# HGRN2 outer-product attention and a PReLU network on one core: where the off-diagonal products are put in PSUM and in TensorE's order

## The chip, the core and the metric

One Trainium2 chip, and one of its cores. A core has a matrix engine (TensorE; in the profile PE for its matmuls and PEld for its weight loads), VectorE (DVE), ScalarE (ACT), GpSimd (POOL) and SyncE (SP), which only issues transfers here. Matmuls write to PSUM, a memory of eight banks with 512 float32 columns each on 128 partitions; VectorE and ScalarE read them from there. Engines run on their own and wait for each other by semaphores. The metric is the time of one launch in microseconds on the device; the kernel before took 618.38 us (median of three runs, 618.32 to 619.0).

## The reference

```python
f = 1.0 / (1.0 + np.exp(-f_logit))
for t in range(S):                                  # S = 768, B, H, D = 4, 8, 48
    state = f[:, :, t, :, None] * state + np.einsum('bhd,bhe->bhde', k[:, :, t], v[:, :, t])
    y[:, :, t] = np.einsum('bhd,bhde->bhe', q[:, :, t], state)
...
x = attn_out.transpose(0, 2, 1, 3).reshape(B * S, H * D)       # 3072 x 384
h = x @ w_in                                                   # 384 x 2048
g = np.maximum(h, 0.0) + alpha * np.minimum(h, 0.0)
return (g @ w_out).astype(np.float32)                          # 2048 x 384
```

The recurrence can be written as a masked matrix of scores within a chunk of time plus a carried state. For a time t and an earlier time s of one chunk the score is q[t]·k[s] times the product of the forget gates between them.

## The kernel before

**Steps.** Time is cut in six chunks of 128, and the batch of four in two pairs. A step is one chunk of one pair, so there are 12 steps (numbered 0 to 11 here); the first two hold the first chunk (`c == 0`), and "from the third step on" means steps 2 to 11 (`c > 0`). Each step has four parts, written as generators: `prepare` (L258, key P or Q), `carry` (L432, key O), `attend` (L506, key S), and `network` (L609, key n), the dense layers on a step's rows.

**Order.** TensorE, VectorE and ScalarE work in exactly the order in which the program writes their instructions. This order is the string at L31 to L37: each key runs the generator of that kind up to its next `yield`. `n` is the network of the step before, `Q` the preparation of the step after. `FIRST` holds the first four steps, `USUAL` the rest. In a usual step TensorE's order is

- the first `S`: scores `raw0` (L520) and `qu0` (L535) of the first batch; two pieces of `n` (12 `ph` matmul instructions each, L618);
- the second `S`: `raw1`, `qu1` of the second batch; one `n`;
- the first `O`: `off` (L444); one `n`; the second `O`: `pd` (L484), the new part of the state; four more `n`;
- `pa`, `pb` (L657, the second dense layer), `py` (L574, the attention's output, in the third to fifth `S`), and the other products of L657.

**Scores.** `raw` has the scores between times of the same or a neighbouring group of four, 80 columns of every 128, `qu` those further apart within a block of 32. VectorE puts both into the tile `ad` with masked copies (four at L526, seven at L541 for each batch), and ScalarE copies `ad` into the big score tile `A` (L563). `off` holds scores between the two blocks of 32 in a half chunk of 64: `kh` (keys scaled to the end of their block, written at L374) against `q3[.., 2]` (queries scaled from the start of theirs, L368). ScalarE copies `off` into `A` with four copies (L462). Four more copies (L419) bring the carried part. `py` multiplies `A` with the values.

**Instructions.** A float32 matmul of the program is two matmuls and two weight loads on the chip: 64 of each for the 32 `off` matmuls of a step, and 64 for a batch's `raw` or `qu`. [...]

**PSUM.** `pair` (L122) hands out two banks at a time from a pool of two such pairs, in turn. A usual step of before asks for seven pairs: raw0, qu0, raw1, qu1, off, pd, py. `network` has four single banks.

**ScalarE and VectorE beside it.** A piece of `n` gives ScalarE one `neg` (L623, reads `ph`) and VectorE two `gate` (L625); every fourth piece adds four `S` (L702). `Q` has on ScalarE L279 to L282, L314 and L419, and on VectorE L290 to L415. The second `O` gives VectorE L494 and L498. On the queues, POOL loads `k`, `q`, `f` and `v` (L266, L276), and SP moves `kt` to `ksn` (L427), which `pd` reads.

Of the kernel before, what the change touches and what calls it, by code (L numbers as in the profile page):

```python
# [18 lines left out]
DB = 32  # L19
MASKED = (1, 0)  # L20

U = 2
CH = 64
NC2 = C // CH
# [6 lines left out]
FIRST = (  # L31
        "P5 a2 P a O w S w a w a2 S Q S O S w Q2 S Q2 S w",
        "a2 w2 n O b w n b2 S P v2 n2 S b v Q n b n O S2 v n b v n Q2 b v Q b n S v2 W Q W S n2 W n",
        "n S P n2 S W n W n O Q n3 O S Q n S Q n Q S2 Q n3",
        "S n3 P S Q S n O n O n4 Q S Q S Q n S Q n Q n2",
)
USUAL = "S n2 S n O n O n Q n3 Q n Q S3 n Q S n Q n Q n"  # L37

def flat(first, usual, steps=12):
    out = []  # L40
# [18 lines left out]
def kernel(  # L59
# [30 lines left out]
    nc = tc.nc  # L90
    B, NC, _, HP, _ = qT.shape
# [7 lines left out]
    W = U * HP * C  # L99
# [13 lines left out]
    QW = QO.pop()  # L113
# [8 lines left out]
    def pair(name):  # L122
        return psa.tile([128, 2, 512], F32, tag="pair", name=name)
# [39 lines left out]
    for m in range(1, NB):  # L163
        lo = UO[m] + (4 if m == 1 else 0)
        n = NB - m
# [4 lines left out]
    for half in range(2):  # L170
        for m in range(1, NQ):
            n = NQ - m
# [7 lines left out]
    A = const.tile([128, U, H, C], F32, tag="A", name="A")  # L180
# [67 lines left out]
    def rows(par):  # L248
        return slice(64 * par, 64 * par + D)
# [182 lines left out]
    def carry(bp, c, x):  # L432

        i = f"{bp}_{c}"
        q3, ks, kh, f64 = (x[n] for n in ("q3", "ks", "kh", "f64"))
        off = pair(f"off_{i}")
        for u in range(U):
            for hp in range(HP):
                for cc in range(NC2):
                    g = (u * HP + hp) * NC2 + cc  # L440
                    o = (u * HP + hp) * DB
                    for par in range(2):
                        r_ = rows(par)
                        nc.tensor.matmul(off[CH * cc:CH * cc + DB, par, o:o + DB],  # L444
                                         lhsT=kh[r_, g], rhs=q3[r_, g, 2], start=True, stop=True)
        if not c:
            for u in range(U):
                for hp in range(HP):
                    for j in range(NJ):
                        g = (u * HP + hp) * NJ + j  # L450
                        o = U * HP * DB + (u * HP + hp) * 16
                        for par in range(2):
                            r_ = rows(par)
                            nc.tensor.matmul(off[DB * j:DB * (j + 1), par, o:o + 16], lhsT=x["k16"][r_, g],
                                             rhs=x["q16"][r_, g], start=True, stop=True)
            for u in range(U):
                o = U * HP * DB + u * HP * 16
                nc.scalar.copy(ad[:, u, :, :, 16:DB], off[:, :, o:o + HP * 16].rearrange("p r (h t) -> p r h t", h=HP))
        for cc in range(NC2):
            s_ = slice(CH * cc, CH * cc + DB)  # L460
            for par in range(2):
                nc.scalar.copy(A[s_, :, par * HP:(par + 1) * HP, CH * cc + DB:CH * (cc + 1)],  # L462
                               off[s_, par, 0:U * HP * DB].rearrange("p (u h t) -> p u h t", u=U, h=HP))


        if not c:
            pk = pair(f"pk_{i}")
            for u in range(U):
                for hp in range(HP):
                    a = (u * HP + hp) * NC2  # L470
                    nc.tensor.transpose(pk[:, u, hp * 128:(hp + 1) * 128], ks[:, a:a + 2].rearrange("p c s t -> p (c s t)"), ident)
            ksn = x["ksn"] = work.tile([128, U, HP * 128], F32, tag="ksn", name=f"ksn_{i}", bufs=1)
            for u in range(U):
                nc.scalar.copy(ksn[:, u], pk[:, u])
        yield
        pd = pair(f"pd_{i}")
        ksn = x["ksn"]
        for u in range(U):
            for hp in range(HP):
                for cc in range(NC2):  # L480
                    for par in range(2):
                        o = (u * HP + hp) * D
                        s_ = halves(cc)[0]
                        nc.tensor.matmul(pd[rows(par), cc, o:o + D],  # L484
                                         lhsT=ksn[s_, u, hp * 128 + 64 * par:hp * 128 + 64 * par + D],
                                         rhs=vs[bp][s_, cc, u, (2 * hp + par) * D:(2 * hp + par + 1) * D], start=True, stop=True)

        def moved(cc):

            of, to = halves(cc)[1], halves(1 - cc)[1]  # L490
            was, then = (vs[bp][p, a, :, 0:DM].rearrange("p u (h e) -> p u h e", e=D)
                         for p, a in ((of, cc), (to, 1 - cc)))
            if c or cc:
                nc.vector.tensor_tensor(then, was, f64[of].unsqueeze(3).broadcast_to((D, U, H, D)), ALU.mult)  # L494
            for par in range(2):
                now = pd[rows(par), cc, 0:U * HP * D].rearrange("p (u h e) -> p u h e", u=U, e=D)
                if c or cc:
                    nc.vector.tensor_tensor(then[:, :, par:H:2], then[:, :, par:H:2], now, ALU.add)  # L498
                else:
                    nc.scalar.copy(then[:, :, par:H:2], now)  # L500

        x["moved"] = moved
        moved(0)
        yield

    def attend(bp, c, x):  # L506

        i = f"{bp}_{c}"
        k, k4, us = (x[n] for n in ("k", "k4", "us"))


        QL, QS = (UW, UW) if c else (VW, C)
        for u in range(U):
            raw = pair(f"raw{u}_{i}")
            for hp in range(HP):
                for j in range(NJ):
                    g = (u * HP + hp) * NJ + j
                    for par in range(2):
                        r_ = rows(par)
                        nc.tensor.matmul(raw[DB * j:DB * (j + 1), par, hp * C:hp * C + QW],  # L520
                                         lhsT=k[r_, g * DB:(g + 1) * DB], rhs=qd[r_, g], start=True, stop=True)
            adu = ad[:, u].rearrange("p r h (i t) -> p (r h) i t", t=4)
            rv = raw.rearrange("p r (h x) -> p (r h) x", h=HP)
            for d in range(4):
                n = 4 - d
                nc.vector.copy_predicated(  # L526
                    adu[:, :, :, d:4], mraw[:, d, :, d:4].bitcast(I32).unsqueeze(1).broadcast_to((128, H, NB, n)),
                    rv[:, :, QO[d]:QO[d] + NB * n].rearrange("p h (i t) -> p h i t", t=n))
            qu = pair(f"qu{u}_{i}")
            for hp in range(HP):  # L530
                for j in range(NJ):
                    g = (u * HP + hp) * NJ + j
                    for par in range(2):
                        r_ = rows(par)
                        nc.tensor.matmul(qu[DB * j:DB * (j + 1), par, hp * QS + 4:hp * QS + QL],  # L535
                                         lhsT=k4[r_, g * DB:(g + 1) * DB], rhs=us[r_, g, 4:QL], start=True, stop=True)
            if c:
                for m in range(1, NB):
                    lo = UO[m] + (4 if m == 1 else 0)
                    n = DB - 4 * m  # L540
                    nc.vector.copy_predicated(  # L541
                        ad[:, u, :, :, 4 * m:DB],
                        mquad[:, lo:lo + n].bitcast(I32).unsqueeze(1).unsqueeze(1).broadcast_to((128, 2, HP, n)),
                        qu[:, :, 0:HP * UW].rearrange("p r (h x) -> p r h x", h=HP)[:, :, :, lo:lo + n])
            else:
                qv = qu.rearrange("p r (h x) -> p (r h) x", h=HP)
                adh = ad[:, u].rearrange("p r h (a t) -> p (r h) a t", a=2)
                for m in range(1, NQ):
                    n = 4 * (NQ - m)
                    lo = 4 if m == 1 else VO[m]  # L550
                    hi = lo + (DB - 4 if m == 1 else 2 * n)
                    to, of, by = ad[:, u].rearrange("p r h t -> p (r h) t")[:, :, 4:DB], qv[:, :, lo:hi], mhalf[:, lo:hi]
                    by = by.bitcast(I32).unsqueeze(1).broadcast_to((128, H, hi - lo))
                    if m > 1:
                        to = adh[:, :, :, 4 * m:16]
                        of, by = (t.rearrange("p h (a t) -> p h a t", a=2) for t in (of, by))
                    nc.vector.copy_predicated(to, by, of)
            yield

        for u in range(U):  # L560
            for j in range(NJ):
                s_ = slice(DB * j, DB * (j + 1))
# [5 lines left out]
        for u in range(U):  # L568
            for hp in range(HP):
                for cc in range(NC2):  # L570
                    for par in range(2):
                        hd = 2 * hp + par
                        o = hp * C + CH * cc
                        nc.tensor.matmul(py[64 * par:64 * par + 64, u, o:o + CH],  # L574
                                         lhsT=vs[bp][:, cc, u, hd * D:hd * D + 64],
# [223 lines left out]
```

## Time and profile before

| what | value |
|---|---|
| median of three runs | 618.38 us |
| span of the profiled execution | 616.6 us |
| instructions | 19078 |
| PE, PEld busy | 587.9 us, 525.1 us |
| DVE, ACT, POOL busy | 496.0 us, 245.7 us, 62.8 us |
| TensorE clock granted | 1.00 in the steps from 100 us on |
| off L444: weight loads, matmuls | 768 each, 102 to 156 ns and 192 to 260 ns long |
| A<-off L462 | 48 copies of 32x256, 360 ns median |
| ad<-mraw,raw L526 | 96 masked copies, 441 ns |
| POOL k L266 waits for PE raw L520 | 208.0 us, 11 times |

The span runs from the first instruction of the program to the last; the median lies 1.8 us above it, for what is around the program in a launch. A busy time counts when an instruction is in flight, so that small matmuls which run side by side count once. The line numbers are those of the kernel before. In the lines that tell of waiting, `<-` names what ended the wait; `issue` means that nothing in the profile was waited for.

### The profile page before, as it was taken

The page shows a single profiled execution, that of the slowest core. Times are in us where ns is not written, and L with a number is a line of the kernel's source. Part 1 is how long each engine was busy: PE and PEld are TensorE (multiplying, and loading weights), DVE is VectorE, ACT ScalarE, POOL GpSimd, SP SyncE. Part 2 cuts the span into 40 slices and gives each one's busy share as a digit, 9 for nine tenths or more (in the row PEclk, how much of TensorE's full clock was granted, in tenths as well). Part 3 has the DMA queues.
Part 4 walks back from the last instruction along what each step waited for, and adds up shares of the span by engine and source line. Part 5 has one row for each costly group of instructions (what it writes and reads, how often), then busy time and mean ns, then how long its engine had stood idle before and what let it go on. Part 6 is the DMA issues. An engine that isn't in the chain of part 4 may idle for free.

```text
span 616.6 us, 19078 instructions
## 1 busy us (share of the span) xinstructions
PE 587.9 (95%) x8220; PEld 525.1 (85%) x8220; DVE 496.0 (80%) x997; ACT 245.7 (40%) x466; POOL 62.8 (10%) x117
## 2 busy tenths in 40 slices
PE   3568999999999999999999999999999999999997
PEld 3457867898899899899889899899889889889997
DVE  7599898899898798798798798798898889762251
ACT  5687852441641361262261261352352343223110
POOL 9120010001010011001001001001001000000000
PEclk9998999999999999999999999999999999999999
DMA  9965532014414214214313313413413301201000
GB/s 302 368 236 180 161 86 54 35 37 120 89 31 75 70 39 105 67 35 98 78 34 93 83 35 90 86 35 87 89 35 86 89 2 27 55 1 27 27 1 26
DMA packets 68116, 50.43 MB, mean 82 GB/s; under 512 B 47168, under 2 KB 60608, under 8 KB 68032
## 3 DMA queue, kind: packets, MB, share of 16 engines
q1 hardware_dynamic: 56656, 25.01, 15.6%
q0 software_dynamic: 6864, 22.35, 13.0%
q10 hardware_dynamic: 4512, 1.85, 1.7%
q8 instruction: 65, 1.06, 0.7%
q14 instruction: 19, 0.16, 0.1%
HBM read 36.21 MB, written 4.72 MB: 66 GB/s over the span
## 4 chain that ended last, share of the span: by engine, by line
PE 67%; DVE 19%; ACT 9%; issue 4%; DMA 1%; ACTq 0%; SPq 0%; DVEq 0%
PE ph L618 27%; PE pc L657 9%; PE pa L657 6%; PE pd L657 5%; PE pe L657 4%; PE po L638 3%; PE raw L520 3%; DVE gate L625 3%; PE qu L535 3%; ACT A L563 3%; DVE S L702 3%; DVE qd L287 3%; PE py L574 3%; ACT us L314 2%; PE pb L657 2%
## 5 line engine op out<-in xcount | busy, mean ns | idle before, releaser
L618 PE MATMUL ph<-xT,w_in_sb 128*128 128x256 f32 x1152 | 261.2, 383 | 0.7 <-DVE Csum L661 0.7
L618 PEld LDWEIGHTS ph<-xT,w_in_sb 128*128 128x128 f32 x1152 | 215.9, 190 | 33.2 <-issue 2.4
L623 ACT ACTIVATE neg<-ph 128x512 f32<-128x512 f32 x96 | 57.2, 596 | 198.2 <-PE ph L618 157.1
L625 DVE SCALAR_TENSOR_TENSOR gate<-neg,om,ph 128x256 f32<-128x256 f32 x192 | 82.3, 477 | 52.3 <-ACT neg L623 52.1
L657 PE MATMUL pc<-t,S 128*128 128x192 f32 x352 | 61.7, 329 | 0.0
L657 PE MATMUL pa<-w_out_sb,gate 128*128 128x192 f32 x352 | 61.3, 327 | 0.1
L657 PEld LDWEIGHTS pa<-w_out_sb,gate 128*128 128x128 f32 x352 | 57.9, 190 | 1.0 <-DVE gate L625 0.4
L657 PEld LDWEIGHTS pc<-t,S 128*128 128x128 f32 x352 | 57.3, 190 | 0.6
L526 DVE COPY_PREDICATED ad<-mraw,raw 128x256 f32<-128x256 int32 (+1 forms) x96 | 42.4, 441 | 10.7 <-PE raw L520 8.2
L541 DVE COPY_PREDICATED ad<-mquad,qu 128x224 f32<-128x224 int32 (+6 forms) x140 | 42.0, 300 | 6.2
L419 ACT COPY A<-q 48x512 f32<-48x512 f32 x44 | 27.2, 617 | 36.4 <-DVE q L368 35.9
L563 ACT COPY A<-ad 32x256 f32<-32x256 f32 x96 | 38.5, 401 | 1.4
L330 DVE TENSOR_TENSOR us<-us,fs 128x768 f32<-128x768 f32 (+5 forms) x60 | 36.7, 612 | 0.0
L678 ACT ACTIVATE o<-pa 128x192 f32<-128x192 f32 x11 | 3.6, 330 | 75.2 <-PE pa L657 65.4
L661 DVE SCALAR_TENSOR_TENSOR Csum<-pc,Csum 128x192 f32<-128x192 f32 x22 | 7.8, 356 | 29.8 <-PE pc L657 29.6
L574 PEld LDWEIGHTS py<-A,vs 128*64 128x64 f32 x768 | 25.7, 145 | 6.1 <-issue 2.8
L702 DVE TENSOR_TENSOR S<-gate 128x512 f32<-128x512 f32 x44 | 30.3, 688 | 0.8
L574 PE MATMUL py<-A,vs 128*64 128x64 f32 x768 | 28.7, 232 | 1.9 <-ACT vs L500 0.9
L657 PE MATMUL pd<-w_out_sb,S 128*128 128x192 f32 x176 | 30.4, 326 | 0.0
L657 PE MATMUL pb<-t,gate 128*128 128x192 f32 x176 | 30.4, 326 | 0.0
L657 PE MATMUL pe<-w_out_sb,S 128*128 128x192 f32 x176 | 30.4, 326 | 0.0
L520 PEld LDWEIGHTS raw<-qd,k 48*32 48x32 f32 x1536 | 18.5, 109 | 13.5 <-issue 11.1
(101 smaller groups left out, 744.3 us busy)
## 6 DMA issues: line engine op xcount, KB each, us to landing
w_out_raw<-in_w_out SPq DMA_DIRECT2D x8, 767.8 KB, 5.3
w_in_raw<-in_w_in SPq DMA_DIRECT2D x8, 767.2 KB, 12.1
q<-in_qT POOLq DMA_DIRECT2D x11, 512.0 KB, 4.2
f<-in_fT POOLq DMA_DIRECT2D x11, 512.0 KB, 4.5
k<-in_kT POOLq DMA_DIRECT2D x11, 512.0 KB, 4.8
out<-o SPq DMA_DIRECT2D x24, 192.0 KB, 3.0
vs<-in_v POOLq DMA_DIRECT2D x22, 192.0 KB, 4.8
ksn<-kt SPq DMA_DIRECT2D x80, 32.0 KB, 2.0
```

What stands on the lines that cost most here:

```text
L330: nc.vector.tensor_tensor(us[:, :, UO[m]:UO[m] + 4 * n].rearrange("p g (i r) -> p g i r", r=4), us[:, :, skip:skip + 4 * n].rearrange("p g ...
L419: nc.scalar.copy(A[halves(cc)[1], :, par * HP:(par + 1) * HP, CH * cc:CH * (cc + 1)], q3[rows(par)].rearrange("p (u h c) s t -> p u h c (s ...
L520: nc.tensor.matmul(raw[DB * j:DB * (j + 1), par, hp * C:hp * C + QW], lhsT=k[r_, g * DB:(g + 1) * DB], rhs=qd[r_, g], start=True, stop=True)
L526: nc.vector.copy_predicated(adu[:, :, :, d:4], mraw[:, d, :, d:4].bitcast(I32).unsqueeze(1).broadcast_to((128, H, NB, n)), rv[:, :, QO[d]: ...
L541: nc.vector.copy_predicated(ad[:, u, :, :, 4 * m:DB], mquad[:, lo:lo + n].bitcast(I32).unsqueeze(1).unsqueeze(1).broadcast_to((128, 2, HP, ...
L563: nc.scalar.copy(A[s_, u, :, s_], ad[s_, u].rearrange("p r h t -> p (r h) t"))
L574: nc.tensor.matmul(py[64 * par:64 * par + 64, u, o:o + CH], lhsT=vs[bp][:, cc, u, hd * D:hd * D + 64], rhs=A[:, u, par * HP + hp, CH * cc: ...
L618: nc.tensor.matmul(ph[:, j * T:(j + 1) * T], lhsT=w_in_sb[:, kt, m * 128:(m + 1) * 128], rhs=xT[:, kt], start=(kt == 0 and j == 0), stop=( ...
L623: nc.scalar.activation(neg, phv, AF.Relu, scale=-1.0)
L625: nc.vector.scalar_tensor_tensor(gate[:, m % NH, m // NH], neg[:, j], om[:, m:m + 1], phv[:, j], ALU.mult, ALU.add)
L657: nc.tensor.matmul(to[:, 0:DH], lhsT=of(f), rhs=by(f), start=(f == 0 and not more), stop=(f == NH - 1), skip_group_check=True)
L702: nc.vector.tensor_tensor(to, x_, y_, op)
```

## The change

From step 2 on `off` has no pair of banks of its own. Directly after the `raw` matmuls of a batch, `attend` issues that batch's 16 `off` matmuls (32 instructions) into the 32 columns behind the 80 that `raw` uses, in the same two banks. The two ScalarE copies of that batch to `A` come after its four masked copies of L526, and each takes 32 x 256 elements as before. `carry` has only one `yield` left in these steps, and the order has one `O` less. Steps 0 and 1 are as they were.

```diff
-        "n S P n2 S W n W n O Q n3 O S Q n S Q n Q S2 Q n3",
-        "S n3 P S Q S n O n O n4 Q S Q S Q n S Q n Q n2",
+        "n S P n2 S W n W n Q n3 O S Q n S Q n Q S2 Q n3",
+        "S n3 P S Q S n2 O n4 Q S Q S Q n S Q n Q n2",
 )
-USUAL = "S n2 S n O n O n Q n3 Q n Q S3 n Q S n Q n Q n"
+USUAL = "S n2 S n2 O n Q n3 Q n Q S3 n Q S n Q n Q n"
...
     def carry(bp, c, x):
...
-        off = pair(f"off_{i}")
...
         if not c:
+            off = pair(f"off_{i}")
+            for u in range(U):
...
+            for cc in range(NC2):
+                s_ = slice(CH * cc, CH * cc + DB)
...
-        yield
+            yield
         pd = pair(f"pd_{i}")
...
     def attend(bp, c, x):
...
+            if c:
+                gap = raw.rearrange("p r (h x) -> p r h x", h=HP)[:, :, :, QW:QW + DB]
+                for hp in range(HP):
+                    for cc in range(NC2):
+                        g = (u * HP + hp) * NC2 + cc
+                        for par in range(2):
+                            r_ = rows(par)
+                            nc.tensor.matmul(gap[CH * cc:CH * cc + DB, par, hp],
+                                             lhsT=kh[r_, g], rhs=q3[r_, g, 2], start=True, stop=True)
...
+            if c:
+                for cc in range(NC2):
+                    s_ = slice(CH * cc, CH * cc + DB)
+                    nc.scalar.copy(A[s_, u, :, CH * cc + DB:CH * (cc + 1)].rearrange("p (r h) t -> p r h t", r=2),
+                                   gap[s_])
```

In `carry` the loops of `off` and of its four copies move unchanged under `if not c`. In `attend` the four masked copies of L526 stand between the two added parts.

## The prediction

> **Forecast: slower, 621.7 us.** I read the page, then TensorE's order of time, then who waits for whom.
>
> **What bounds it now.**
>
> ```profile
> span 616.6 us, 19078 instructions
> ...
> PE 587.9 (95%) x8220; PEld 525.1 (85%) x8220; DVE 496.0 (80%) x997; ACT 245.7 (40%) x466; POOL 62.8 (10%) x117
> ...
> q8 instruction: 65, 1.06, 0.7%
> ```
>
> TensorE is the bound. The last line will matter: a queue brings instructions, 65 packets, 1.06 MB, so 16 KB each; TensorE's 16,440 instructions and 248 waits, over 65, make 257 instructions per packet. TensorE in step 7, by time (start, length, what):
>
> ```profile
> 339.47 5.45 PE L618 MATMUL ph<-xT,w_in_sb 128*128 128x256 f32 x24
> 344.85 0.92 PE L520 MATMUL raw<-qd,k 48*32 48x80 f32 x64
> 345.54 1.07 PE L535 MATMUL qu<-us,k 48*32 48x112 f32 x64
> 346.54 2.86 PE L618 MATMUL ph<-xT,w_in_sb 128*128 128x256 f32 x12
> 349.32 0.76 PE L444 MATMUL off<-q,kh 48*32 48x32 f32 x64
> 350.01 2.86 PE L618 MATMUL ph<-xT,w_in_sb 128*128 128x256 f32 x12
> 352.80 1.22 PE L484 MATMUL pd<-vs,ksn 64*48 64x48 f32 x64
> ```
>
> One section starts as the last ends, nothing is waited for.
>
> **The gain in a usual step.** By starts, 12 `ph` take 2.78 us on either side of `off`, 24 in one piece 5.38: joining them saves 2.78 + 2.79 - 5.38 = 0.19. `off` costs 350.01 - 349.32 = 0.69. Behind `raw` its 64 matmuls cost 64 times the pace of a small matmul in a stream: 9.0 ns (between the starts of `off` itself), 10.9 (`raw`, 0.69/64), 15 (`qu` in the first half of a step, its slowest). That is 0.58, 0.70 or 0.96; I take 0.61, near `off`'s own row. Net 0.19 + 0.69 - 0.61 = 0.27 gained per step; ends -0.08 and +0.30.
>
> **Does it reach the end?** Yes in steps 4 to 11. From the fourth `gate` on, VectorE and ScalarE set the pace up to `py` (TensorE idles there 0.2 to 0.4 us), but that stretch starts with a wait for TensorE:
>
> ```profile
> 353.58 0.87 DVE L625 SCALAR_TENSOR_TENSOR gate<-neg,om,ph 128x256 f32<-128x256 f32 x2 [2.16 <-ACT neg L623]
> ```
>
> The gain lies ahead of it, so the stretch moves too. Eight steps: 8 x 0.27 = 2.15.
>
> **The copies on ScalarE** keep their count and size. What waits is new. Whether they may read beside L526 the trace can't show; if not, the second batch's start when L526 ends, about 348.5 in step 7, and take 4 x 0.36 / 2 = 0.72. Behind them queues `neg` of the next `ph`, due at 349.8: 0.5 to spare, or 2 if they may. `raw1` needs the first pair free at 345.1 and has it at 342.1; `pd` needs the second at 352.5 and has it at 349.3. L526 itself waits 0.3 longer for `off`, under the `gate` before it. The removed pair leaves every reuse as far away as it was. No transfer is added; SP and POOL keep their order, and `k`'s load (behind raw1) moves with TensorE. In one step `pd` waited 0.29 for `ksn`, which `py`'s idle time swallowed (`py` 2.08 instead of 2.37). All this I cost at 0; should the `neg` be late by x, TensorE loses x less the 2.16 of the row above.
>
> [...]
>
> **Steps 2 and 3 are different.** VectorE's waits from 110.5 to 150 us, and TensorE's from 100 (sum, times, longest):
>
> ```profile
> DVE gate L625 <- ACT neg L623: 1.3, 1, 1.3
> ```
>
> ```profile
> PE ph L618 <- DVE Csum L661: 0.7, 1, 0.7
> ```
>
> VectorE waits for TensorE once, before the third `gate` (110.62), then never; TensorE waits for it at the end. `off` (116.92) lay under that stretch. Now half of it is ahead of the third `ph`: +0.29, all on the path. In step 3 ScalarE's two copies stand before L279 to L282, which feed L287; VectorE is then 0.5 later, eats the 0.5 that the gate before `pa` has to spare, and most of that step's gain: -0.1 (ends -0.6, +0.1).
>
> **The cost: TensorE outruns its instructions.** In the first steps nothing hides it. Weight loads of step 0:
>
> ```profile
> 26.32 0.34 PEld L520 LDWEIGHTS raw<-qd,k 48*32 48x32 f32 x20 [1.27 <-issue]
> 26.50 0.17 PEld L535 LDWEIGHTS qu<-us,k 48*32 48x32 f32 x2
> 26.54 0.17 PEld L520 LDWEIGHTS raw<-qd,k 48*32 48x32 f32 x1
> 26.55 0.13 PEld L535 LDWEIGHTS qu<-us,k 48*32 48x32 f32 x1
> 26.60 0.19 PEld L520 LDWEIGHTS raw<-qd,k 48*32 48x32 f32 x4
> 26.63 1.08 PEld L535 LDWEIGHTS qu<-us,k 48*32 48x32 f32 x61
> 29.23 0.75 PEld L520 LDWEIGHTS raw<-qd,k 48*32 48x32 f32 x38 [1.52 <-issue]
> 32.24 0.34 PEld L520 LDWEIGHTS raw<-qd,k 48*32 48x32 f32 x21 [2.27 <-issue]
> ```
>
> It stops in the middle of `raw`, waiting for nothing. From one such stop (26.32) to the next (32.24) go 127 pairs and 2 waits: 256 instructions, one packet. Step 1 again, in the 128 loads of L454 behind `off`:
>
> ```profile
> 51.57 0.57 PEld L454 LDWEIGHTS off<-us 48*32 48x32 f32 x53 [1.46 <-issue]
> ```
>
> Three packets and no other stop lie between. The trace's list of DMA packets has the ones that ended the three stops: they started at 23.57, 29.77, 48.88 and took 1.28, 1.11, 1.40; TensorE went on 1.3 to 1.5 after each. So a block of 256 is fetched when the one before is entered: some 0.6 to 1.1 us until its packet starts, 0.9 to 1.5 for the packet, 1.37 after it, 3.3 in all. A block of small matmuls alone lasts 1.4. A stream of 256 (`raw`, `qu`) always has `ph` in its block; one of 320 can hold a whole block. Counting on from 51.57 in blocks of 256, in the new order:
>
> - Step 2, first batch: a block starts at the 60th instruction of `raw0`, the next 256 later, six before `qu0` ends. Its packet stands in the trace: 103.96, 1.29 long, usable at 106.6. TensorE is there at 102.77 + 0.70 + 0.29 + 0.78 = 104.5: stop of 2.1, ahead of the third `ph`, so in full.
> - Step 5, second batch: block start at the 72nd of `raw1`; stop 3.7 - 2.4 = 1.3 after it.
> - Step 10, second batch: at the 63rd; 3.6 - 1.8 = 1.8.
>
> Elsewhere TensorE's sequencer enters the block under `ph`, some 36 instructions ahead, or `ph` fills it. Ends: 0 (the fetch keeps up) and 5 stops of 1.7 (steps 3 and 7, whose starts lie within 16 instructions of such a place, too).
>
> [...] The stops at 26.32, 32.24 and 51.57, one block each, speak for a single block ahead.
>
> **Sum.** +0.29 + 2.1 (step 2) - 0.1 (step 3) - 2.15 + 1.3 + 1.8 = +3.3 on 616.6: span 619.9. The median lies 1.8 above the span: 618.4 + 3.3 = **621.7**.
>
> **Rivals.**
>
> 1. The fetch keeps up: +0.29 - 0.1 - 2.15 = -2.0: **616.4**, faster. For it: no such stop from step 2 on in the trace of before, in 20 streams. Against: none of those streams holds a whole block. It decides while a packet is usable within 1.4 us of entry. 13 in 100.
> 2. Only step 2 stops, since later blocks lie otherwise (waits added to TensorE's queue shift them): +0.29 + 2.1 - 0.1 - 2.15 = +0.1: **618.5**. The count holds to step 2, where the code is the old one; further on each wait moves it by one. 15 in 100.
> 3. The joined `ph` bring nothing in steps 4 to 11, since VectorE's stretch binds whole steps: +0.29 + 2.1 - 0.1 + 3.1 = +5.4: **623.8**. Against: its 2.16 of waiting in each step. With it more stops, five: 621.7 + 2 x 1.7 = 625.1. 17 in 100.
>
> The forecast has 55 in 100, with its own range 620.2 to 623.5. The whole range reaches down to rival 2 and up past 3's first time: 617.9 to 624.6. Within 0.2% (1.24 us, about what a measurement tells from no change) lies rival 2 and a little of the others: 0.16; faster, rival 1: 0.14; slower 0.70.
>
> **What would show it.** After: L444 only in steps 0 and 1 (128); in step 2 a gap of 2 us, released by `issue`, near the end of `qu0`; two more of 1 to 2 us inside or just behind long streams; in the other steps `ph` in blocks of 24 from `qu1` to `pd`, each step 0.27 shorter. Wrong if no such gap shows, or if ScalarE's copies make `gate` wait.

## The result, and the profile after

The median of the changed kernel is 625.65 us (four runs, 624.1 to 627.51) beside 618.35 for the kernel before, a ratio of 1.0124 (95% interval 1.0103 to 1.0146): slower, as forecast, but by 7.3 us and not by 3.3, and outside the range, which ended at 624.6. In the profiled execution the span is 7.6 longer. The page of the kernel after, its lines on busy time and on the queue that brings instructions (packets, MB, share):

```profile
span 624.2 us, 19088 instructions
...
PE 589.5 (94%) x8220; PEld 527.7 (85%) x8220; DVE 496.4 (80%) x997; ACT 248.0 (40%) x466; POOL 63.0 (10%) x117
...
q8 instruction: 65, 1.06, 0.8%
```

The work is the same to the instruction on every engine, and TensorE is busy for 1.6 us more while the span grows by 7.6. So TensorE idles. Its waits from 95 to 625 us (sum, times, longest):

```profile
PE qu L549 <- issue: 4.9, 3, 1.7
PE py L588 <- ACT A L577: 1.1, 6, 0.3
PE ph L632 <- DMA ksn<-kt: 0.7, 1, 0.7
...
```

The first line is new: three times TensorE stops inside `qu` (L549 now) and waits for nothing that the profile shows. The third line is a fourth such stop, in step 7: `ph` does not read `ksn`, and a transfer of it happened to end then. The weight loads show where they stand (start, length, what, idle time before), in steps 2, 5, 7 and 10:

```profile
104.04 0.78 PEld L549 LDWEIGHTS qu<-us,k 48*32 48x32 f32 x59
106.68 0.14 PEld L549 LDWEIGHTS qu<-us,k 48*32 48x32 f32 x4 [1.85 <-issue]
...
258.33 0.10 PEld L549 LDWEIGHTS qu<-us,k 48*32 48x32 f32 x1 [1.95 <-issue]
...
345.50 0.73 PEld L632 LDWEIGHTS ph<-xT,w_in_sb 128*128 128x128 f32 x4 [0.17 <-issue]
347.26 1.81 PEld L632 LDWEIGHTS ph<-xT,w_in_sb 128*128 128x128 f32 x9 [1.03 <-DMA ksn<-kt]
...
497.07 0.14 PEld L549 LDWEIGHTS qu<-us,k 48*32 48x32 f32 x5 [1.81 <-issue]
```

The prediction had the first "six before `qu0` ends"; four pairs come after it. Counting weight loads, matmuls and TensorE's waits, all four stops stand at the same place modulo 256, to within one instruction, which is also that of the three stops in the first two steps from which the prediction counted. And each ends 1.2 to 1.6 us after the end of an instruction packet in the trace's list of DMA packets: the one ahead of the first stop started at 104.06 and took 1.33, and TensorE went on at 106.68.

Windows around the first one (us; TensorE's busy time and matmuls, the loads, VectorE, ScalarE, POOL; then the granted clock, share and rate of DMA):

```profile
103.10:107.00 3.90, 2.28 (x161) 1.87 (x160) 2.55 (x6) 1.03 (x3) 0.00 (x0) 0.98 0.44 118
107.00:114.00 7.00, 7.00 (x26) 5.62 (x24) 2.97 (x9) 3.27 (x6) 0.00 (x0) 0.76 0.01 4
```

Behind the stop the clock is not 1.00 but 0.76 on average: the record has it at one half for 3.41 us from 106.9. The 24 `ph` in that stretch take 6.97 us instead of 5.38.

An undisturbed step is as forecast in its shape. Step 6, matmuls, from the second batch's scores to `pd`:

```profile
303.70 0.85 PE L519 MATMUL raw<-qd,k 48*32 48x80 f32 x60
...
304.40 0.47 PE L529 MATMUL raw<-q,kh 48*32 48x32 f32 x29
304.73 1.09 PE L549 MATMUL qu<-us,k 48*32 48x112 f32 x64
305.75 5.45 PE L632 MATMUL ph<-xT,w_in_sb 128*128 128x256 f32 x24
311.12 0.94 PE L483 MATMUL pd<-vs,ksn 64*48 64x48 f32 x64
```

`off` (L529) stands between `raw` and `qu`, and the 24 `ph` are one piece. By the starts of its sections, the step is only 0.18 shorter than in the kernel before.

From these starts the 7.6 us split as follows (us; the stop of step 2 is what its first scores are longer than its second; those of steps 5, 7 and 10 are the change of the whole step, plus the 0.144 by which the five steps without a stop are shorter on average).

| term | predicted | measured |
|---|---|---|
| ahead of step 2 | 0 | +0.31 |
| step 2, half of `off` ahead of the third `ph` | +0.29 | +0.33 |
| step 2, stop | +2.1 | +1.94 |
| step 2, halved clock behind it (6.97 - 5.38) | none | +1.59 |
| step 3 | -0.1 | -0.05 |
| steps 4 to 11 without their stops, 8 x 0.144 | -2.15 | -1.15 |
| step 5, stop | +1.3 | +1.97 |
| step 10, stop | +1.8 | +1.77 |
| step 7, stop | 0 | +0.93 |
| sum | +3.3 (the terms make 3.24) | +7.6 |

### The profile page after: what moved, and what is told of

It reads as the page before. It is cut to its first block, busy times and chain, and to the rows that moved or that the text cites. A ratio compares the mean times of both kernels' runs of the same rounds, so it can differ in the third digit from the quotient of the medians.

```text
span 624.2 us, 19088 instructions
## 1 busy us (share of the span) xinstructions
PE 589.5 (94%) x8220; PEld 527.7 (85%) x8220; DVE 496.4 (80%) x997; ACT 248.0 (40%) x466; POOL 63.0 (10%) x117
## 4 chain that ended last, share of the span: by engine, by line
PE 60%; DVE 23%; ACT 11%; issue 4%; DMA 2%; SPq 0%; ACTq 0%; DVEq 0%
PE ph L632 25%; PE pc L671 9%; PE pa L671 5%; DVE gate L639 4%; PE pd L671 4%; ACT A L577 4%; PE pe L671 4%; DVE S L716 4%; PE po L652 3%; DVE qd L287 3%; ACT us L314 3%; PE qu L549 3%; PE raw L519 3%; PE py L588 2%; ACT neg L637 2%
## 5 line engine op out<-in xcount | busy, mean ns | idle before, releaser
L535 DVE COPY_PREDICATED ad<-mraw,raw 128x256 f32<-128x256 int32 (+1 forms) x96 | 42.5, 443 | 11.1 <-PE raw L519 6.8
L541 ACT COPY A<-raw 32x256 f32<-32x256 f32 x40 | 14.5, 363 | 50.6 <-DVE ad L535 50.4
L549 PE MATMUL qu<-us,k 48*32 48x112 f32 (+1 forms) x1536 | 27.7, 259 | 4.9 <-issue 4.9
## 6 DMA issues: line engine op xcount, KB each, us to landing
w_in_raw<-in_w_in SPq DMA_DIRECT2D x8, 767.2 KB, 10.9
```

Of the source, the lines that this page charges most:

```text
L535: nc.vector.copy_predicated(adu[:, :, :, d:4], mraw[:, d, :, d:4].bitcast(I32).unsqueeze(1).broadcast_to((128, H, NB, n)), rv[:, :, QO[d]: ...
```

## The experiments

Theory A is the prediction's: blocks of 256 instructions are fetched one ahead, and a stream of small matmuls that holds a whole block uses it up before the next has come. Rival B: the stream itself, or two tiles in one bank, stops TensorE, wherever blocks begin. To leave out the start, where times differ from run to run, the time from `raw0` of step 2 to the end is compared: 513.8 in the profile of before, 521.1 in that of after.

### Moving the blocks, not the work

The start has a loop of small matmuls that keep TensorE running while the first data comes. Each is four instructions on the chip (56 of them make 112 weight loads and 112 matmuls at L736 in the trace of before), so more of them move every later block.

```diff
-IDLE = 56
+IDLE = 64
```

(`e1_pad32` from the kernel after, `e3_before_pad32` from the kernel before; `e2_pad136` has 90 there, in the kernel after.)

> The changed kernel with 8 more idle matmuls at the very start, where TensorE waits for data anyway: 32 instructions more ahead of everything, so that every block of 256 instructions begins 32 instructions earlier in the program. Measured: the time from the start of raw0 in step 2 to the end of the span (before 616.6 - 102.8 = 513.8 us, after 624.2 - 103.1 = 521.1). Theory A (TensorE stops because a block of 256 instructions is used up before the next has come): the stops leave steps 2, 5 and 10; worked out from the trace of after with a block usable 3.7 us after TensorE's sequencer enters the one before, one of 1.2 us is left in step 7 (in or behind the first batch) and one of 0.6 in step 9; 514.8, and 1.6 more for each stop that is followed by a halved clock; median about 619.5. Rival B (the long stream of small matmuls, or the shared bank, stops TensorE by itself, wherever blocks begin): the stops stay in steps 2, 5, 7 and 10, 521 us, median 625.7.

Measured: 514.9 us from `raw0` to the end, median 619.88, ratio 1.0025 (1.0014 to 1.0035). TensorE's waits, as above:

```profile
PE qu L549 <- issue: 1.0, 1, 1.0
...
PE ph L632 <- issue: 0.3, 1, 0.3
```

Steps 2, 5 and 10 have no stop. Two smaller ones are left, in the first batch of step 7 (its scores 3.31 instead of 2.1 to 2.2) and in the `ph` behind the second batch of step 9 (5.95 instead of 5.38): 1.2 and 0.6, the steps and sizes that were worked out. Eight matmuls more at the start bring back 5.8 of the 7.3 us; B is refuted.

> The changed kernel with 34 more idle matmuls at the start, 136 instructions. Theory A: stops in the second batch of step 2 (2.0 us), the first batch of step 5 (1.4), the first of step 10 (0.8), and 0.5 in step 7: 513 + 4.7 = 517.7 us from raw0 of step 2 to the end, and 1.6 more if the clock is halved behind the first; median about 622 to 624. Rival B: first batch of step 2, second batches of steps 5 and 10, first of step 7, as in after: 521 us, 625.7.

Measured: 516.1 us, median 628.43, ratio 1.0153 (1.0124 to 1.0182). The stops are in the second batch of step 2 (scores 3.82 instead of 2.0), the first batch of step 5 (4.15 instead of 2.15), the first of step 10 (2.57) and in step 7 (`ph` 5.60): the four places of A, with 1.8, 2.0, 0.4 and 0.2 for 2.0, 1.4, 0.8 and 0.5. No clock was halved from step 2 on. The median is 4 to 6 us over the expectation; the profiled execution was the shortest of six (623.57 to 630.29), so where the others lost their time was not seen. The expected places hold, the expected median does not.

> The kernel before with the same 32 instructions more at the start, the control. Theory A and rival B: its streams of small matmuls are 256 instructions at most, so no stop from step 2 on wherever the blocks begin; 513.8 +- 0.4 us from raw0 of step 2 to the end. The stops of steps 0 and 1 may shift, so the median may move by 1 to 2 us either way. If instead stops of 1 us or more appear from step 2 on, then the size of the stream is not what protects the kernel before.

Measured: 513.4 us from `raw0` to the end, median 617.68, ratio 1.0001 (0.9986 to 1.0016). No wait for `issue` stands among TensorE's waits from step 2 on; the longest is that of before:

```profile
PE ph L618 <- DVE Csum L661: 0.7, 1, 0.7
```

### The length alone, and the work without the length

`e10_before_longer` gives the kernel before streams of 320 instructions, without a shared bank and without moving `off`. The loop is that of `raw`:

```diff
-            for hp in range(HP):
+            for hp in [*range(HP)] + [0, 1] * bool(c):
```

> The kernel before with its streams made longer and nothing else: from step 2 on the first 16 of a batch's 32 raw matmuls are issued a second time with the same data (64 instructions), so that raw and qu make 320 in one piece, as in the change; off keeps its own banks and its place. Theory A, by the trace of before with 3.7 us from entry to use: stops of 2.0 us at the end of the first batch of step 2, 1.9 in the first batch of step 5 and 1.9 in the second batch of step 10, none over 0.5 elsewhere; with 10 x 0.72 for the doubled matmuls 513.8 + 7.2 + 5.8 = 526.8 us from raw0 of step 2 to the end, and 1.6 more if the clock is halved behind the first. Rival B: no stop, 521.

Measured: 525.6 us from `raw0` to the end, median 630.63, ratio 1.0197 (1.0162 to 1.0233). Weight loads that follow more than 0.35 us of idling:

```profile
106.23 0.14 PEld L535 LDWEIGHTS qu<-us,k 48*32 48x32 f32 x4 [1.72 <-issue]
...
249.80 0.14 PEld L535 LDWEIGHTS qu<-us,k 48*32 48x32 f32 x5 [1.75 <-issue]
...
499.42 0.15 PEld L535 LDWEIGHTS qu<-us,k 48*32 48x32 f32 x7 [1.27 <-issue]
```

These are the first batches of steps 2 and 5 and the second of step 10, and no others: three places worked out from the trace of before, each somewhat shorter than 1.9 to 2.0. Length is enough.

`e9_split` does the opposite: all of the change, but a piece of `ph` inside each long stream.

```diff
                                    gap[s_])
+                yield
...
-USUAL = "S n2 S n2 O n Q n3 Q n Q S3 n Q S n Q n Q n"
+USUAL = "S n S n S n S n O n Q n3 Q n Q S3 n Q S n Q n Q n"
```

(The two special steps are cut in the same way.)

> The changed kernel with each long stream cut in two: a piece of ph between raw with off (192 instructions) and qu (128), so the shared columns, the moved matmuls and the number of instructions are those of the change, and only the length of a stream is not. Theory A: no stop over 0.5 us from step 2 on. The price of the cut: no ph piece is joined any more, and one break of ph more per step than in the kernel before (0.19), off at its in-stream price of 0.75 instead of 0.69: 0.25 per step longer than before, 513.8 + 2.5 = 516.3 us from raw0 of step 2 to the end, median 620.5. Rival B (sharing or moving off is what stops TensorE): stops as in after, 522 or more.

Measured: 518.7 us, median 624.04, ratio 1.0096 (1.0059 to 1.0133). TensorE's waits from step 2 on:

```profile
PE ph L633 <- DVE Csum L676: 1.3, 1, 1.3
PE py L589 <- ACT A L578: 1.0, 5, 0.3
PE pa L672 <- DVE gate L640: 0.2, 1, 0.2
```

No stop is left, so the shared columns and the moved matmuls make no stop by themselves. The price of the cut was expected too low: a usual step is 47.7 us, 0.35 over before instead of 0.25, and step 3 alone takes 50.0 instead of 48.2, with the 1.3 us wait for VectorE in the first line.

### The change without stops

`e5_no_stop` moves the blocks at the start and four times more, so that none falls into a stream. The doubled `pd` matmuls write the same values again.

```diff
-IDLE = 56
+IDLE = 63
...
+        more = {(0, 2): 2, (0, 3): 5, (0, 4): 6, (0, 5): 5}.get((bp, c), 0)
+        again = [(0, 0, n // 2 % 2, n % 2) for n in range(more)]
+        for u, hp, cc, par in again + [(u, hp, cc, par) for u in range(U) for hp in range(HP)
...
```

> The changed kernel with its blocks laid so that none falls into a long stream: 7 idle matmuls more at the start (28 instructions), and in steps 4, 6, 8 and 10 the first 2, 5, 6 and 5 pd matmuls issued twice with the same data (8, 20, 24 and 20 instructions). Places worked out from the trace of after with 3.7 us from entry of a block to the next one's use. Theory A: no stop over 0.5 us from step 2 on; what is left is the change's own worth, with the steps' lengths of after and e1_pad32 that had no stop: 512.9 us from raw0 of step 2 to the end (before 513.8, after 521.1), median about 617.4. Rival B (some of the loss of after is not the blocks but the streams themselves): 515 or more, median 619.5 or more.

Measured: 512.8 us from `raw0` to the end, median 617.53, ratio 1.0002 (0.9991 to 1.0012). All that TensorE waits for from step 2 on, where a wait for `issue` no longer stands:

```profile
PE pa L671 <- DVE gate L639: 0.5, 2, 0.2
PE py L588 <- ACT A L577: 0.5, 2, 0.3
PE ph L632 <- DVE Csum L675: 0.4, 1, 0.4
```

So the whole loss is the stops and what follows them. The change's own worth is 1.0 us by the profile, and no difference that the times can show.

### Once more as it is

`e6_after_again` is the changed kernel, not edited.

> The changed kernel as it is, a second profile and more times, to see what belongs to it in every execution. Theory A: the four stops at the same four places (2.0, 2.0, 1.0, 1.9 us within 0.5); the halved clock directly behind the stop of step 2 (1.6 us) only in some executions, so that the time is 624 to 625 without it and 626 to 627.5 with it. Rival E: the halved clock follows that stop every time.

Measured: median 626.26 (625.24 to 629.15). The four stops are in the same places: the loads of steps 2 and 5 and of 10 idle for up to 2.31, and `ph` in step 7 takes 6.20. The clock is again halved for 3.41 us behind the first, from 106.7. Seven more runs of this kernel have only a time and a mean clock. Two with 0.995, the value of both profiles (626.04 and 626.26 us), took 626.15 and 626.82. Two with 0.999 and 1.000 took 624.1 and 625.27; 3.41 us at one half would make 0.997 of them. So it comes in some executions, and they are 1 to 3 us longer, about as expected; rival E falls as far as a mean clock can tell. These times don't price it alone, since the two runs without it also lack the half clock at the start that both profiles have; in the profiles the `ph` behind the stop cost 1.59 and 1.35 us more. Of the other three, 0.997 (625.24 us) leaves open where the clock was halved, and 0.975 and 0.978 (629.15 and 627.51) had more of it than the profiles, at places not seen.

### The joined `ph` without the long stream

`e4_off_beside_pd` is the kernel before with `off` in its own banks, directly ahead of `pd`.

```diff
-USUAL = "S n2 S n O n O n Q n3 Q n Q S3 n Q S n Q n Q n"
+USUAL = "S n2 S n2 O2 n Q n3 Q n Q S3 n Q S n Q n Q n"
```

(Steps 2 and 3 likewise.)

> The kernel before with only its order changed: from step 2 on off and pd are issued one directly behind the other, with no ph between them, so that the ph pieces around off are joined as in the change, but off keeps its own banks and no stream is longer than before. Theory A with the prediction's price of a join (0.19 us for each, ten steps): 513.8 - 1.9 = 511.9 us from raw0 of step 2 to the end, median 616.5. Rival C (joining ph saves nothing): 513.8, median 618.4. Rival D (the change from tiles of 48x32 to tiles of 64x48 costs 0.3 us where nothing of full size lies between): 515, median 619.5.

Measured: 517.0 us, median 622.07, ratio 1.0059 (1.0046 to 1.0072). Step 7, matmuls by time:

```profile
348.00 5.45 PE L618 MATMUL ph<-xT,w_in_sb 128*128 128x256 f32 x24
353.38 0.76 PE L444 MATMUL off<-q,kh 48*32 48x32 f32 x64
354.24 1.58 PE L484 MATMUL pd<-vs,ksn 64*48 64x48 f32 x64
```

The 24 `ph` again take 5.38 by starts, so the join is worth its 0.19. But from step 3 on `off` to `pd` takes 0.82 to 0.98 instead of 0.69, and `pd` 1.42 to 1.57 instead of 0.87: its first 16 loads take 0.23 us for every four, where the kernel before takes 0.04. That is 0.8 more, of which `py`, which used to wait 0.3 for ScalarE, takes back 0.3. Rival D has the sign, with 517.0 for its 515. Whether it is the change of tile size that spreads these loads was not tried.

### A version that beats both

The prediction says that VectorE and ScalarE set the pace up to `py`. `e7_copies_early` takes that wait away in the kernel before: the copies of `ad` into `A` (L563) go where ScalarE idles.

```diff
-USUAL = "S n2 S n O n O n Q n3 Q n Q S3 n Q S n Q n Q n"
+USUAL = "S n2 S n S O n S O n Q n3 Q n Q S n Q S n Q n Q n"
```

> The kernel before with only its order changed in steps 4 to 11: the two batches' copies of ad into A on ScalarE (3.3 us) no longer directly ahead of py, but behind the second batch's scores, where ScalarE idles. TensorE's order is unchanged. If py (2.3 to 2.4 us) is held up by these copies alone, it falls to 2.05 and each of the eight steps is 0.3 shorter: 511.3 us from raw0 of step 2 to the end, median 615.8. If VectorE holds it as well: no change, 618.3.

Measured: 511.1 us, median 615.72, ratio 0.9967 (0.9955 to 0.9980). ScalarE in step 6:

```profile
302.09 1.64 ACT L563 COPY A<-ad 32x256 f32<-32x256 f32 x4
303.75 1.27 ACT L462 COPY A<-off 32x256 f32<-32x256 f32 x4
305.04 0.60 ACT L623 ACTIVATE neg<-ph 128x512 f32<-128x512 f32 x1
305.66 1.64 ACT L563 COPY A<-ad 32x256 f32<-32x256 f32 x4
```

The two groups of L563 now stand around the copies of `off`, and TensorE in the same step:

```profile
321.40 2.09 PE L574 MATMUL py<-A,vs 128*64 128x64 f32 x64
```

`py` is one piece of 2.02 by starts in all eight steps, where it took 2.1 to 2.4. This is faster than both kernels.

> e5_no_stop with the copies moved as in e7_copies_early. If both hold and add: 512.9 - 2.5 = 510.4 us from raw0 of step 2 to the end, median 614.9. If a wait fewer on TensorE moves the blocks, one or two stops of 0.5 to 2 us come back: up to 617.

(The order of L37 is here "S n2 S n S n S O n Q n3 Q n Q S n Q S n Q n Q n".) Measured: 511.7 us, median 616.45, ratio 0.9977 (0.9962 to 0.9992): faster than before, not faster than `e7_copies_early`. `py` is 2.02, but 1.3 of the expectation is missing. Step 9 has 0.54 of it: `pd` takes 1.41 there instead of 0.87, and 0.28 are in step 5, where it takes 1.15. Ahead of a `py` that waits such a delay costs nothing; here nothing is left to take it up.

## Why the prediction was right and wrong

**Right: what decides.** The cause, the sign and three of the places were named. Moved blocks move the stops (`e1_pad32`, `e2_pad136`), length alone makes them (`e10_before_longer`), and streams cut below 256 instructions have none (`e9_split`). Four stops of 0.93 to 1.97 us at one place modulo 256 agree with the prediction's single block of 256 instructions ahead.

**Right: the rows of a usual step.** `ph` around `off`, 6.27 us by starts, became 5.38: the 0.19 + 0.69 of the prediction. ScalarE's copies wait for the masked copies (L526, now L535), the dearer of the two cases; the group of these copies on the page of after (busy us, mean ns, idle time before and what ended it):

```profile
L541 ACT COPY A<-raw 32x256 f32<-32x256 f32 x40 | 14.5, 363 | 50.6 <-DVE ad L535 50.4
```

All but 0.2 of the idling ahead of them is ended by VectorE, and it costs nothing, as predicted: none of TensorE's waits names `gate` or `neg` in a usual step, and `pd` stays at 0.87.

**Right: steps 2 and 3.** The third `gate` begins 4.19 us later (114.81, was 110.62) and `raw0` of step 3 also 4.19: what comes ahead of that `gate` goes through in full. Step 3 gained 0.05 for 0.1.

**Wrong: "Behind `raw` its 64 matmuls cost 64 times the pace of a small matmul in a stream ... I take 0.61, near `off`'s own row."** Over steps 4 to 11 the scores of a step take 4.26 us in `e5_no_stop` (2.14 + 2.12) and 3.53 before (1.79 + 1.74): 0.73, 11.4 ns each. That is near the row of `raw`, 10.9, behind which it stands, and not the 9.0 of `off` on its own. The gain per step was 0.15 and not 0.27; 1.0 us of the miss.

**Wrong: "Elsewhere TensorE's sequencer enters the block under `ph` ... or `ph` fills it."** Step 7, one of the two near misses that were named, held some 248 instructions of one block in its stream, and stopped for 0.93 in the `ph` behind it. Step 5's stop was 1.97, not 1.3: by the trace of after its block begins at about the 64th instruction of `raw1` and not at the 72nd, so it ends inside `qu1` and not behind four `ph`, which take 0.22 us each. A count that is off by a few instructions is off by tenths of a microsecond in such a stop. Together the two are 1.6 us of the miss. The end of the range, five stops of 1.7, had allowed for more than that, but the range was cut short of it.

**Wrong by leaving out: a stop is not over when TensorE goes on.** The 3.41 us at half clock behind the stop of step 2, 1.59 us in the profiled execution, is in no term and in no end of the range. The trace of before could have warned: its clock record has one such stretch, from 52.0 us, behind the stop of step 1.

**The rivals.** Rival 1 and 2 fall with the four stops. Rival 3's time (623.8, or 625.1 with five stops) was nearest, by a wrong reason: the joined `ph` do bring their 0.19, and no VectorE stretch holds whole steps.

## What to carry to other kernels

Before lengthening a run of small instructions, count the engine's instructions between pieces of long work: as long as no run held a whole block of 256 instructions, where blocks began made no difference here (from step 2 on, before: 513.8 and 513.4 us with two alignments); from then on an edit far ahead of it can move the time by microseconds (after: 514.9 to 521.8 us with three). Price an instruction that moves into a stream by the stream's row, not by its own (here 11.4 ns, near the 10.9 of `raw`, and not the 9.0 of `off`). And where an engine waits a little at the end of each step, remove that wait first: here it was worth more (513.8 - 511.1 = 2.7 us by the profiles) than the change without its stops (1.0).

## What the runs showed of the hardware

Where in a stream a block began decided here whether it stopped. Counted in the profiles of after, `e1_pad32`, `e2_pad136` and `e10_before_longer`, all 13 stops of 0.2 us or more stand where the block begins between about the 37th and the 78th instruction of a stream of 320, and no stream with a block's start there is without one; each ends 1.2 to 1.6 us after the end of an instruction packet. Blocks that begin at the 1st to 32nd instruction lie wholly in the stream too, and show no stop. In steps 6, 8 and 11 of after, where such a block lies in a stream, the next packet started 1.5 to 2.3 us before the stream's first matmul (301.43 for 303.70 in step 6); in the four streams that stop it started 0.9 to 1.2 us after it.

A stop in a stretch that is otherwise busy can be followed by half of TensorE's clock. In both profiles of the changed kernel the half clock lasts 3.41 us and begins where a window of 3.41 us ends (on the grid of the clock's records: those of after begin at 42.03, 52.27, 55.68, 106.88 and 110.30, which is 3, 4, 19 and 20 times 3.413 behind the first) in which TensorE had idled for 1.62 and 1.96 us. Idle time in a window does not settle it alone: 1.49 us in step 2 of `e10_before_longer` and 1.60 in step 5 of `e6_after_again` left the clock at 1.00, while at the start 1.42 us before 52.0, in the kernel before, were enough. What else counts was not tried.
